# One fused attention and two-MoE kernel: a batch's attention cut in two token halves, weight preparation and two small routing pieces put at other places of the order

## The chip, the cores and the metric

The kernel runs on one core of a Trainium2 chip. The metric is the device time of one execution, in microseconds (us). The same launch holds all three parts of the reference, so there is one time for all of it. PE is the matrix engine (TensorE), DVE the vector engine, ACT the scalar engine, POOL is GpSimd, and SP is the engine whose queue issues most transfers. Every engine works off its instructions in the order in which the program lists them; what comes later on an engine waits behind what comes earlier.

## The reference

Three stages follow each other. Attention reads 4 batches of 8 heads with 512 tokens and 32 state rows of 64 numbers; the tokens read the state and the state reads the tokens:

```
scores  = scale * x @ state^T     a  = softmax(scores)     xread = a  @ state
scores2 = scale * state @ x^T     a2 = softmax(scores2)    sread = a2 @ x
x = concat([xread, sread], tokens)          # 4 * 544 = 2176 rows of 8*64 = 512
```

The first mixture of experts has 8 experts of width 1024. Its weights P come from a gate after 8 rounds of row and column scaling over all 2176 rows, and every expert works on every row:

```
out = sum over e of P[:, e] * (relu(x @ w1[e]) @ w2[e])
```

The second mixture takes that result. Every row goes to the one expert of its largest gate logit, and the result is scaled by that expert's softmax value and by a sigmoid of a second gate. Everything is float32.

## The kernel before

All matrix products that need float32 precision are made of two parts: a number is written as hi + lo (both in a reduced format, fp32r), and a product is three matmuls, hi·hi, hi·lo and lo·hi. The hi part is a copy on ACT, the lo part a subtraction on DVE or POOL.

**The first mixture** takes most of the time: 3 passes over the rows (768, 768 and 640 of them, held transposed in `xst`), each of 32 steps. A step `s` is a quarter of one expert. `mm1(s)` is a product of two 2×2 block matrices in seven block products instead of eight (p1 to p7; L483 to L485 are the three matmuls of each), and needs seven operands of `x` (`XR`, made once for a pass by `xsplit`, L405 to L407, of four sums that `xsums` makes, L390 to L393) and seven of the weights (made for each step by `prep_w1`: f0 are four sums on POOL, L433 to L436, and two copies on ACT, L437 and L438; f1 is a cast on ACT, L441, and the lo parts on POOL, L443 to L448, and then the load of the next step's quarter of W1). `prep_w2` casts the step's quarter of W2 (ACT L458), makes its lo part (POOL L461, in two pieces) and then issues the next quarter's load. The results of `mm1` are summed from PSUM on DVE (L509 to L533), made positive on ACT (L492) and split on DVE (L496). `mm2` multiplies these by W2 (L565 to L567) and adds to `acc` (DVE L583).

**The start-up** comes before step 0. The first pass needs the first 768 columns of the transposed attention result, which is all of batch 0 and the first 256 tokens of batch 1. The start-up computes batches 0 and 1 entirely, in five links for each batch and each half of the heads: c1 transposes x (PE L202, copies ACT L205 and DVE L207), c2 makes scores (PE L213; DVE, ACT), c3 scales (DVE L230 to L233), c4 transposes the result (PE L238, copy ACT L240) and c5 multiplies with the state (PE L250; copies into `xst` at L254 and, for the columns that belong to the second pass, into `xtm` at L256, from where they go to DRAM). Between the links, and between the block products of step 0, PE runs products of ones (`idle_work`, L138), which compute nothing that is used.

**A queue** holds what is left of the attention (batches 2 and 3, the reads of the states, the gate L310 of each row tile), and then the row and column scaling (`sinkhorn`). `pump` takes items from it at fixed places of the steps: each place brings as much credit as the PE work there lasts, and an item costs `pace`. So the list's order and `pace` set at which place of which step an item's instructions stand on every engine. ACT, DVE, POOL and SP get them at the same places.

**The second mixture** begins behind the third pass. `sel_a` (L731 to L750) is an item of the queue in the third pass and works out on DVE which rows go to the first two slots. The tail runs slots: `m1`, `hT` (transposes; copies L877 on ACT and the lo part L878 on DVE), `m2s` (L885 to L887; result scaled on DVE L891 and scattered by POOL L892). `split_w` splits the next slot's weights (ACT L810, DVE L811 of 128x2048 each). `Rq[3][2]` and `Rq[4][2]` are the small operations of `fc` (L697 to L708, 11 each), `gmul` makes `osg` of their result on POOL (L1208, two operations), and `gtab` (PE L719, then DVE L1216) multiplies by it; `gt` scales the results of slots from 2 on.

The order within each engine is written by hand: the body stands under `tc.manual_schedule()`, so the order of the calls is the order of the instructions.

Of the kernel before, what the change touches and what calls it, by code (L numbers as in the profile page):

```python
# [21 lines left out]
def tile_state_attention_moe_moe2(  # L22
# [166 lines left out]
    def attention(b, g):  # L189
# [3 lines left out]
        def c1():  # L193
            xb = xbs.pop((b, g))
            if b == 1:
                T["xT"] = acc.rearrange("p a c -> p (a c)")[:, 1024 * g : 1024 * g + 1024].rearrange("p (a s) -> p a s", a=2)
            else:
                T["xT"] = ap2.tile([P, 2, S], F32, tag="xT", name=f"xT{n}")
            for pl in range(2):
                ps = bank(f"psx{n}{pl}")  # L200
                for r in range(R):
                    nc.tensor.transpose(ps[:, r * P : (r + 1) * P],  # L202
                                        xb[:, r, 2 * pl : 2 * pl + 2, :].rearrange("p h d -> p (h d)"), ident)
                if pl == 0:
                    nc.scalar.copy(T["xT"][:, pl, :], ps)  # L205
                else:
                    nc.vector.tensor_copy(T["xT"][:, pl, :], ps)  # L207

        def c2():
            ps = bank(f"pss{n}")  # L210
            for pl in range(2):
                for r in range(R):
                    nc.tensor.matmul(ps[:, r * P + 64 * pl : r * P + 64 * pl + 64],  # L213
                                     T["xT"][:, pl, r * P : (r + 1) * P],
                                     sbds[b][:, g, 64 * pl : 64 * pl + 64], start=True, stop=True)
            m1 = ap2.tile([P, 16], F32, tag="m1", name=f"m1{n}")
            v = ps.rearrange("p (a s) -> p a s", s=NS)
            nc.vector.tensor_reduce(out=m1, in_=v, axis=AX.X, op=ALU.max)
            e1 = ap2.tile([P, S], F32, tag="e1", name=f"e1{n}")
            ev = e1.rearrange("p (a s) -> p a s", s=NS)  # L220
            nc.vector.tensor_tensor(out=ev, in0=v, in1=m1.unsqueeze(2).to_broadcast([P, 16, NS]), op=ALU.subtract)
            nc.scalar.activation(out=e1, in_=e1, func=AF.Exp, scale=SCALE)
            s1 = ap2.tile([P, S], F32, tag="s1", name=f"s1{n}", bufs=4)
            nc.scalar.copy(s1, ps)
            T["s1"], T["e1"] = s1, e1

        def c3():
            d1 = ap2.tile([P, 2, 16], F32, tag="d1", name=f"d1{n}")
            ev = T["e1"].rearrange("p (a s) -> p a s", s=NS)
            nc.vector.tensor_reduce(out=d1[:, 0, :], in_=ev, axis=AX.X, op=ALU.add)  # L230
            nc.vector.tensor_scalar_add(d1[:, 0, :], d1[:, 0, :], EPS)
            nc.vector.reciprocal(d1[:, 1, :], d1[:, 0, :])
            nc.vector.tensor_tensor(out=ev, in0=ev, in1=d1[:, 1, :].unsqueeze(2).to_broadcast([P, 16, NS]), op=ALU.mult)  # L233

        def c4():
            ps = bank(f"psa{n}")
            for r in range(R):
                nc.tensor.transpose(ps[:, r * P : (r + 1) * P], T["e1"][:, r * P : (r + 1) * P], ident)  # L238
            T["aT"] = T["xT"][:, 1, :]
            nc.scalar.copy(T["aT"], ps)  # L240

        def c5():

            c0 = b * S
            n1 = max(0, min(S, 2 * HW - c0))
            if n1 < S:
                xm = xtm[b, g] = ap2.tile([P, 2, S], F32, tag="xtm", name=f"xtm{n}")
            for pl in range(2):
                po = bank(f"pso{n}{pl}")
                nc.tensor.matmul(po, stps[b][64 * pl : 64 * pl + 64, g, :], T["aT"][64 * pl : 64 * pl + 64, :],  # L250
                                 start=True, stop=True)
                kt = 2 * g + pl
                if n1 > 0:
                    nc.scalar.copy(XT1[:, kt, c0 : c0 + n1], po[:, 0:n1])  # L254
                if n1 < S:
                    nc.vector.tensor_copy(xm[:, pl, n1:], po[:, n1:])  # L256
            if n1 < S:
                o = c0 + n1 - 2 * HW
                nc.sync.dma_start(out=xtd[:, 2 * g : 2 * g + 2, o : o + S - n1], in_=xm[:, :, n1:])
# [1023 lines left out]
```

## Time and profile before

| what | value |
|---|---|
| median of 3 runs | 1806.25 us (1804.05 to 1806.64) |
| the profiled execution's own time | 1801.52 us |
| span of its trace | 1799.8 us |
| PE busy | 1770.6 us, 98% |
| DVE, POOL, ACT busy | 67%, 63%, 36% |
| granted PE clock, mean | 0.996 |

The span is the time from the first to the last instruction in the trace; 1.7 us of the execution's own time lie around it. A granted clock of 1.00 is 2.4 GHz and one of 0.50 is 1.2 GHz. In a timeline a row gives start, duration, engine, line, operation, operands and shape; xN says that N of them follow each other, and the bracket says how long the engine was idle ahead of it and what ended that. A matmul's duration includes its passage through the array, so matmuls overlap: the distance of two starts is what one costs.

### The profile page before, as it was taken

The page shows a single profiled execution, that of the slowest core. Times are in us where ns is not written, and L with a number is a line of the kernel's source. Part 1 is how long each engine was busy: PE and PEld are TensorE (multiplying, and loading weights), DVE is VectorE, ACT ScalarE, POOL GpSimd, SP SyncE. Part 2 cuts the span into 40 slices and gives each one's busy share as a digit, 9 for nine tenths or more (in the row PEclk, how much of TensorE's full clock was granted, in tenths as well). Part 3 has the DMA queues.
Part 4 walks back from the last instruction along what each step waited for, and adds up shares of the span by engine and source line. Part 5 has one row for each costly group of instructions (what it writes and reads, how often), then busy time and mean ns, then how long its engine had stood idle before and what let it go on. Part 6 is the DMA issues. An engine that isn't in the chain of part 4 may idle for free.

```text
span 1799.8 us, 25885 instructions
## 1 busy us (share of the span) xinstructions
PE 1770.6 (98%) x9415; PEld 1579.6 (88%) x9415; DVE 1202.5 (67%) x2054; ACT 654.3 (36%) x1114; POOL 1126.4 (63%) x1045
## 2 busy tenths in 40 slices
PE   8999999999999999999999999999999999999998
PEld 6888999999999889999999999889999998778886
DVE  6667589976666786666666666896666666635232
ACT  4433333333333433333333334333333334336333
POOL 2643566876866766666668776787878887311212
PEclk9999999999999999999999999999999999999999
DMA  5342222222222322222232223242222222434122
GB/s 123 89 111 85 79 69 71 71 74 93 68 71 68 122 70 70 70 61 69 71 100 71 71 69 96 71 141 83 82 82 83 82 76 77 138 115 176 43 92 86
DMA packets 126620, 154.67 MB, mean 86 GB/s; under 512 B 41424, under 2 KB 91600, under 8 KB 123920
## 3 DMA queue, kind: packets, MB, share of 16 engines
q1 hardware_dynamic: 122560, 142.55, 25.3%
q0 software_dynamic: 3280, 10.23, 1.8%
q8 instruction: 76, 1.25, 0.3%
q14 instruction: 64, 0.52, 0.1%
q10 hardware_dynamic: 640, 0.13, 0.0%
HBM read 138.99 MB, written 14.42 MB: 85 GB/s over the span
## 4 chain that ended last, share of the span: by engine, by line
PE 77%; issue 10%; DMA 5%; DVE 4%; POOL 2%; ACT 1%; SPq 0%; POOLq 0%; DVEq 0%; ACTq 0%
PE py L565 13%; PE py L566 13%; PE py L567 13%; PE p L483 11%; PE p L485 11%; PE p L484 11%; DMA out_dram<-xst,si 2%; DMA out_dram<-y,si 2%; PE psr L288 1%; PE psg L310 1%; DVE acc L583 1%; POOL wl L461 1%; DMA xb<-in_x_dram 1%; PE pl L612 0%; DVE HB L496 0%
## 5 line engine op out<-in xcount | busy, mean ns | idle before, releaser
L461 POOL TENSOR_TENSOR wl<-rawb,wh 128x512 fp32r<-128x512 f32 x192 | 247.5, 1311 | 395.3 <-ACT wh L458 393.7
L483 PE MATMUL p<-XR 128*128 128x384 f32 (+1 forms) x1344 | 443.7, 330 | 2.6 <-DVE acc L583 2.3
L484 PE MATMUL p<-XR 128*128 128x384 f32 (+1 forms) x1344 | 439.6, 327 | 4.5 <-POOL XR L407 3.9
L485 PE MATMUL p<-XR 128*128 128x384 f32 (+1 forms) x1344 | 439.7, 327 | 0.8 <-POOL XR L448 0.8
L565 PE MATMUL py<-wh,HB 128*128 128x512 f32 x1088 | 428.3, 394 | 1.0 <-DVE u L515 0.8
L567 PE MATMUL py<-wh,HB 128*128 128x512 f32 x1088 | 425.0, 391 | 0.0
L566 PE MATMUL py<-wl,HB 128*128 128x512 f32 x1088 | 424.9, 391 | 0.0
L583 DVE SCALAR_TENSOR_TENSOR acc<-py,PG,acc 128x512 f32<-128x512 f32 x461 | 320.3, 739 | 53.0 <-PE py L567 52.3
L448 POOL TENSOR_TENSOR XR<-sst,XR 128x512 fp32r<-128x512 f32 x192 | 273.6, 1445 | 31.1 <-ACT XR L441 29.8
L484 PEld LDWEIGHTS p<-XR 128*128 128x128 f32 x1344 | 253.2, 188 | 8.8 <-POOL XR L407 4.3
L483 PEld LDWEIGHTS p<-XR 128*128 128x128 f32 x1344 | 253.1, 188 | 7.8 <-DVE acc L583 2.7
L485 PEld LDWEIGHTS p<-XR 128*128 128x128 f32 x1344 | 252.9, 188 | 1.4 <-POOL XR L448 1.4
L565 PEld LDWEIGHTS py<-wh,HB 128*128 128x128 f32 x1088 | 204.4, 188 | 43.2 <-DVE u L515 0.9
L567 PEld LDWEIGHTS py<-wh,HB 128*128 128x128 f32 x1088 | 204.2, 188 | 43.3
L496 DVE SCALAR_TENSOR_TENSOR HB<-u,HB 128x384 fp32r<-128x384 f32 (+1 forms) x192 | 161.8, 845 | 119.1 <-ACT HB L492 118.9
L566 PEld LDWEIGHTS py<-wl,HB 128*128 128x128 f32 x1088 | 204.4, 188 | 38.7
L501 ACT COPY u<-p 128x384 f32<-128x384 f32 (+1 forms) x96 | 44.3, 461 | 462.0 <-PE p L485 461.9
L443 POOL TENSOR_TENSOR XR<-rawb,XR 128x512 fp32r<-128x512 f32 x96 | 140.3, 1461 | 0.4 <-ACT XR L437 0.4
L441 ACT CAST XR<-sst 128x1024 fp32r<-128x1024 f32 x96 | 100.7, 1048 | 101.2 <-POOL sst L436 101.1
L492 ACT ACTIVATE HB<-u 128x384 fp32r<-128x384 f32 (+1 forms) x192 | 96.8, 504 | 77.3 <-DVE u L528 72.1
L509 DVE TENSOR_TENSOR u<-p,u 128x384 f32<-128x384 f32 (+1 forms) x96 | 51.2, 533 | 93.5 <-PE p L485 93.5
L492 ACT ACTIVATE HB<-p 128x384 fp32r<-128x384 f32 (+1 forms) x96 | 45.4, 473 | 164.5 <-PE p L485 164.5
(304 smaller groups left out, 2492.0 us busy)
## 6 DMA issues: line engine op xcount, KB each, us to landing
rawb<-in_moe_w_dram SPq DMA_DIRECT2D x192, 512.0 KB, 3.5
raw<-in_moe_w_dram SPq DMA_DIRECT2D x15, 1024.0 KB, 7.9
xb<-in_x_dram SPq DMA_DIRECT2D x60, 128.0 KB, 3.5
rawb<-in_moe_w_dram SPq DMA_DIRECT2D x5, 1024.0 KB, 5.1
x1d<-acc SPq DMA_DIRECT2D x16, 256.0 KB, 4.3
xtd<-xtm SPq DMA_DIRECT2D x4, 512.0 KB, 2.7
x1p<-acc SPq DMA_DIRECT2D x8, 256.0 KB, 4.3
xst<-xtd SPq DMA_DIRECT2D x1, 1536.0 KB, 9.4
```

Of the source, the lines that this page charges most:

```text
L443: nc.gpsimd.tensor_tensor(out=wop(s, 1, 0, 2).rearrange(r, k=KD), in0=raw[:, :, 0:P], in1=wop(s, 0, 0, 2).rearrange(r, k=KD).bitcast(F32), ...
L448: nc.gpsimd.tensor_tensor(out=wop(s, 1, 3 + i, 2), in0=sst[:, i : i + 2, :].rearrange("p a c -> p (a c)"), in1=wop(s, 0, 3 + i, 2).bitcast ...
L461: nc.gpsimd.tensor_tensor(out=lo[:, c], in0=raw[:, c], in1=hi[:, c].bitcast(F32), op=ALU.subtract)
L483: nc.tensor.matmul(ps, wh, xh, start=start and k == 0, stop=False, skip_group_check=True)
L484: nc.tensor.matmul(ps, wh, xl, start=False, stop=False, skip_group_check=True)
L485: nc.tensor.matmul(ps, wl, xh, start=False, stop=stop and k == 1, skip_group_check=True)
L492: nc.scalar.activation(out=hh[:, f, half * h : (half + 1) * h], in_=c, func=AF.Relu)
L496: nc.vector.scalar_tensor_tensor(out=hl[:, f, q], in0=c, scalar=0.0, in1=hh[:, f, q].bitcast(F32), op0=ALU.max, op1=ALU.subtract)
L565: nc.tensor.matmul(ps, hh[:, j, r], whi[:, j, :], start=(j == 0), stop=False)
L566: nc.tensor.matmul(ps, hh[:, j, r], wlo[:, j, :], start=False, stop=False)
L567: nc.tensor.matmul(ps, hl[:, j, r], whi[:, j, :], start=False, stop=(j == 1))
L583: nc.vector.scalar_tensor_tensor(out=a, in0=ps, scalar=PG[:, t, e : e + 1], in1=a, op0=ALU.mult, op1=ALU.add)
```

## The change

Five edits.

1. `attention` is written as parts over ranges of tokens. Batch 1 is cut in two halves; the start-up computes only the first half of its tokens, and the second half's ten closures stand at the head of the queue, before batch 2. For that x of batch 1 is loaded a second time at the end of the start-up, in place of batch 2, whose load has become part of queue items, as has the state of batch 3. The gates are taken in another order.
2. The start-up and step 0 have another order. Before: `w1b` (the second half of `prep_w1(0)`) behind A1[3]; now between A0[2] and A1[2]. Both halves of `prep_w1(1)` now stand in step 0 or before it, and `prep_w2(0)` at the place 5 of step 0 and not at the place 1. One lo part of `x` (operand 3) moves from POOL to DVE. There are 12 more products of ones in the start-up and 4 fewer in step 0.
3. The pace of the queue is 108 over its 74 items, before 104 over 64.
4. `sel_a` is cut in two items of the queue, `sel_a` and `sel_a2`.
5. In the tail `Rq[3][2]`, `Rq[4][2]` and `gmul` are called behind `hT(1)`; before, they stood inside `m2s(0)`.

```diff
-    def attention(b, g):
+    def attention(b, g, cuts=(0, R)):
...
+        def part(r0, r1):
+            Q = {}
+            nr = r1 - r0
+            w, c = nr * P, slice(r0 * P, r1 * P)
...
+            def c1():
+                xb = xbs.pop((b, g))
+                if b == 1 and r0 == 0:
+                    xt = accf[:, 1024 * g : 1024 * g + 1024]
                 else:
+                    xt = ap2.tile([P, 2 * S], F32, tag="xT", name=f"xT{m}")
...
+        reads = [part(r0, r1) for r0, r1 in zip(cuts, cuts[1:])]
...
-        pool = (3, 1, 6) if p > 0 else (3, 2)
+        pool = (3, 1, 6) if p > 0 else (2,)
...
+        sel.update(o1=o1, tw=tw, es=es)
+
+    def sel_a2():
+        o1, tw = sel["o1"], sel["tw"]
...
-                crit[b, g], lag[b, g] = attention(b, g)
+
+                reads, lag[b, g] = attention(b, g, (0, R) if b != 1 else (0, R // 2, R))
+                crit[b, g] = reads[0]
+                late[b, g] = reads[-1]
...
-        idle_work(6)
+        idle_work(8)
         C0[0]()
+        idle_work(4)
         C1[0]()
         w1a, w1b = prep_w1(0)
         w1a()
         A0[2]()
+        w1b()
         A1[2]()
         C0[1]()
-        idle_work(4)
+        idle_work(10)
         A0[3]()
         idle_work(6)
         A1[3]()
-        w1b()
         C1[1]()
...
-        early = {0: [parts[2], parts[3]], 4: [sums[2]], 1: [parts[4], sums[3]], 2: [parts[5], parts[6]]}
+        ahead_w1 = prep_w1(1)
+        ahead_w1[0]()
+        early = {0: [parts[2]], 4: [parts[3], ahead_w1[1], parts[5]], 1: [sums[2], parts[4], sums[3]], 2: [parts[6]]}
...
-            ahead = s > 0 and s % NU == 0
+            ahead = s % NU == 0
...
-                    idle_work((4, 4, 4, 4, 12, 4, 0)[i])
-                if i == 1 and not ahead:
+                    idle_work((4, 4, 4, 4, 8, 4, 0)[i])
+                if i == (1 if s > 0 else 5) and (s == 0 or not ahead):
                     prep_w2(s)
...
-            load_x(2, g)
+            load_x(1, g)
         load_state(2)
-        load_state(3)
...
-        queue += spread(window(2), [6, 7, 0, 1, 2, 3, 4, 5], 2)
+        h0, h1 = late[1, 0], late[1, 1]
+        queue += spread([h0[0], h1[0], h0[1], seq(lambda: load_x(2, 0), h1[1]), h0[2], seq(lambda: load_x(2, 1), h1[2]),
+                         h0[3], h1[3], h0[4], seq(h1[4], lambda: load_state(3))], [0, 1, 2, 3], 2)
+        queue += spread(window(2), [6, 7, 4, 5], 2)
...
-        pace[0] = 104.0 / len(queue)
+        pace[0] = 108.0 / len(queue)
...
-        m2s(0, (None,) * 6 + (btab, seq(lambda: gather(2), Rq[3][2], Rq[4][2], gmul)))
+        m2s(0, (None,) * 6 + (btab, lambda: gather(2)))
         hT(1)
+        Rq[3][2]()
+        Rq[4][2]()
+        gmul()
         gather(3)
```

Three places show what this does to the order of an engine. The changed file has more lines, so a line of before has another number after: L407 is L424, L433 to L436 are L450 to L453, L443 to L448 are L460 to L465, L458 is L475, L461 is L478, L492 is L509, L501 is L518, L811 is L832, L878 is L899, L891 is L912.

First POOL, from the first sums of W1 (`sst`) on. `wl` is the lo part of W2, `XR` with `sst` or `rawb` beside it the lo parts of W1, `XR` with `acc` or `xst` beside it the lo parts of x. Before:

```order
L433 TENSOR_TENSOR sst<-rawb 128x256
...
L443 TENSOR_TENSOR XR<-rawb,XR 128x512
L445 TENSOR_TENSOR XR<-rawb,XR 128x256
L448 TENSOR_TENSOR XR<-sst,XR 128x512 x2
L407 TENSOR_TENSOR XR<-acc,XR 128x768
L461 TENSOR_TENSOR wl_522<-rawb,wh_521 128x512 x2
L407 TENSOR_TENSOR XR<-xst,XR 128x768
L433 TENSOR_TENSOR sst<-rawb 128x256
```

And after, from the same place on:

```order
L450 TENSOR_TENSOR sst<-rawb 128x256
...
L465 TENSOR_TENSOR XR<-sst,XR 128x512 x2
L450 TENSOR_TENSOR sst<-rawb 128x256
...
L465 TENSOR_TENSOR XR<-sst,XR 128x512 x2
L424 TENSOR_TENSOR XR<-xst,XR 128x768
L478 TENSOR_TENSOR wl_556<-rawb,wh_555 128x512 x2
L478 TENSOR_TENSOR wl_590<-rawb,wh_589 128x512 x2
```

The lo part of `acc` has left POOL, the lo part of `xst` stands ahead of W2's and no longer behind it, and all of step 1's W1 work stands ahead of both.

Then ACT, from the end of step 0 into step 1. `wh` is the cast of a quarter of W2 (the first is step 0's, the second step 1's), `HB` the hi parts of mm1's results, `xT` the transposed x of an attention link. Before:

```order
L492 ACTIVATE HB<-c_106 128x384
L492 ACTIVATE HB<-u_105 128x384
L441 CAST XR<-sst 128x1024
L492 ACTIVATE HB<-u_104 128x384
L501 COPY u_103<-p_1_598 128x384
L458 CAST wh_614<-rawb 128x1024
L437 CAST XR<-rawb 128x512
L438 CAST XR<-rawb 128x256
L205 COPY xT_647<-psx_648 128x512
```

And after:

```order
L509 ACTIVATE HB<-c_106 128x384
L509 ACTIVATE HB<-u_105 128x384
L475 CAST wh_555<-rawb 128x1024
L509 ACTIVATE HB<-u_104 128x384
L518 COPY u_103<-p_1_573 128x384
L475 CAST wh_589<-rawb 128x1024
L215 COPY xT_2_595<-psx_20_596 128x256
L215 COPY xT_2_612<-psx_20_613 128x256
```

Step 0's cast of W2 has come down to the end of step 0, step 1's is behind it by two instructions, and two copies of the new queue items stand right behind that.

Last DVE in the tail. Before (`xst` from `pY` is the result of slot 0, `HB` the lo part of slot 1's `hT`, `setb` the lo part of slot 2's weights):

```order
L705 TENSOR_TENSOR rt_g<-rt_mx,rt_s 128x2
L707 CAST gsplit<-rt_g 128x2
L708 TENSOR_TENSOR gsplit<-rt_g,gsplit 128x2
L891 TENSOR_SCALAR xst<-pY_14162,gt 128x512
L878 TENSOR_TENSOR HB<-pt_0_14242,HB 128x512
L878 TENSOR_TENSOR HB<-pt_1_14249,HB 128x512
...
L811 TENSOR_TENSOR setb_14270<-rawb,HB 128x2048
```

And after:

```order
L912 TENSOR_SCALAR xst<-pY_14227,gt 128x512
L899 TENSOR_TENSOR HB<-pt_0_14282,HB 128x512
L899 TENSOR_TENSOR HB<-pt_1_14289,HB 128x512
L714 TENSOR_REDUCE rt_s<-rt_d 128x3
L715 TENSOR_SCALAR rt_s<-rt_s 128x3
...
L724 CAST gsplit<-rt_g 128x2
L725 TENSOR_TENSOR gsplit<-rt_g,gsplit 128x2
L832 TENSOR_TENSOR setb_14335<-rawb,HB 128x2048
L714 TENSOR_REDUCE rt_s<-rt_d 128x3
L715 TENSOR_SCALAR rt_s<-rt_s 128x3
...
L724 CAST gsplit<-rt_g 128x2
L725 TENSOR_TENSOR gsplit<-rt_g,gsplit 128x2
L832 TENSOR_TENSOR setb_14335<-rawb,HB 128x2048
L714 TENSOR_REDUCE rt_s<-rt_d 128x3
L715 TENSOR_SCALAR rt_s<-rt_s 128x3
...
L724 CAST gsplit<-rt_g 128x2
L725 TENSOR_TENSOR gsplit<-rt_g,gsplit 128x2
L832 TENSOR_TENSOR setb_14335<-rawb,HB 128x2048
```

The 22 operations of the two `fc` stood ahead of these rows and now stand behind them, ahead of the first L832 of slot 2's weights.

## Rows read from the trace of the kernel before

**Rows 1.** The page, busy time of the engines (share of the span, instructions).

```profile
PE 1770.6 (98%) x9415; PEld 1579.6 (88%) x9415; DVE 1202.5 (67%) x2054; ACT 654.3 (36%) x1114; POOL 1126.4 (63%) x1045
```

**Rows 2.** Waits of PE by tile, line and releaser; total us, times, longest.

```profile
PE p L484 <- POOL XR L407: 3.9, 1, 3.9
PE pY L887 <- DVE HB L878: 3.7, 2, 3.4
PE p L483 <- DVE acc L583: 2.3, 2, 1.9
```

**Rows 3.** Timeline of PE, 0 to 50 us.

```profile
32.34 1.99 PE L250 MATMUL pso<-acc,stp 64*128 64x512 f32 x8
34.26 0.44 PE L483 MATMUL p<-XR 128*128 128x384 f32 x1
```

**Rows 4.** Timeline of PE, 50 to 80 us.

```profile
53.71 0.52 PE L483 MATMUL p<-XR 128*128 128x384 f32 x1
...
57.62 0.33 PE L483 MATMUL p<-XR 128*128 128x384 f32 x1
...
58.66 1.03 PE L202 MATMUL psx<-ident,xb 128*128 128x128 f32 x8
...
73.20 1.90 PE L213 MATMUL pss<-sbd,xT 128*128 128x64 f32 x16
```

**Rows 5.** Timeline of POOL, 14 to 75 us.

```profile
27.64 2.95 POOL L448 TENSOR_TENSOR XR<-sst,XR 128x512 fp32r<-128x512 f32 x2 [6.96 <-ACT XR L441]
38.78 1.87 POOL L407 TENSOR_TENSOR XR<-acc,XR 128x768 fp32r<-128x768 f32 x1 [8.20 <-ACT XR L405]
43.41 3.92 POOL L461 TENSOR_TENSOR wl<-rawb,wh 128x512 fp32r<-128x512 f32 x2 [2.75 <-ACT wh L458]
47.29 1.80 POOL L407 TENSOR_TENSOR XR<-xst,XR 128x768 fp32r<-128x768 f32 x1
```

**Rows 6.** Timeline of DVE, 26 to 66 us.

```profile
34.58 0.95 DVE L390 TENSOR_TENSOR acc<-xst 128x768 f32<-128x768 f32 x1
...
38.88 2.59 DVE L392 TENSOR_TENSOR acc<-xst 128x768 f32<-128x768 f32 x1
```

**Rows 7.** Timeline of ACT, 34 to 66 us.

```profile
42.29 1.04 ACT L458 CAST wh<-rawb 128x1024 fp32r<-128x1024 f32 x1
...
51.74 0.52 ACT L492 ACTIVATE HB<-u 128x384 fp32r<-128x384 f32 x1 [3.93 <-DVE u L528]
...
59.30 0.59 ACT L205 COPY xT<-psx 128x512 f32<-128x512 f32 x1 [0.71 <-PE psx L202]
```

**Rows 8.** The page, weight quarter loads: queue, count, size, us to landing.

```profile
rawb<-in_moe_w_dram SPq DMA_DIRECT2D x192, 512.0 KB, 3.5
```

**Rows 9.** Timeline of DVE, 1146 to 1158 us.

```profile
1153.55 2.05 DVE L583 SCALAR_TENSOR_TENSOR acc<-py,PG,acc 128x512 f32<-128x512 f32 x3
```

**Rows 10.** Timeline of DVE, 1562 to 1584 us.

```profile
1563.49 0.17 DVE L697 TENSOR_REDUCE rt_s<-rt_d 128x3 f32<-128x24 f32 x1
...
1568.16 1.28 DVE L878 TENSOR_TENSOR HB<-pt,HB 128x512 fp32r<-128x512 f32 x2
1569.66 2.29 DVE L811 TENSOR_TENSOR setb<-rawb,HB 128x2048 fp32r<-128x2048 f32 x1 [0.23 <-issue]
```

**Rows 11.** Timeline of POOL, 1562 to 1584 us.

```profile
1567.47 1.71 POOL L1208 TENSOR_TENSOR osg<-sm,gsplit 128x408 fp32r<-128x408 bf16 x2 [3.14 <-DVE gsplit L707]
```

**Rows 12.** Timeline of PE, 1563 to 1584 us.

```profile
1575.63 1.97 PE L719 MATMUL pgat<-osg,ohj 128*128 128x48 f32 x17
...
1579.59 0.58 PE L862 MATMUL pm<-HB,XR 128*128 128x512 f32 x1
```

**Rows 13.** Three stretches: length, busy time (instructions) by engine, clock, DMA, GB/s.

```profile
47.20:54.00 6.80, 4.86 (x16) 4.37 (x17) 1.33 (x4) 1.98 (x3) 6.72 (x8) 0.51 0.23 77
1154.40:1157.00 2.60, 2.60 (x14) 2.30 (x15) 2.50 (x6) 0.00 (x0) 2.52 (x3) 1.00 0.28 106
1579.00:1583.00 4.00, 4.00 (x11) 2.84 (x12) 2.34 (x2) 2.23 (x2) 1.74 (x2) 0.61 0.81 306
```

More of the change, by code (lines that the diff above doesn't have):

```diff
@@ L187, in tile_state_attention_moe_moe2 @@
     xtm = {}
-    def attention(b, g):
+    accf = acc.rearrange("p a c -> p (a c)")
+    def attention(b, g, cuts=(0, R)):
         n = f"{b}{g}"
         T = {}
[L193 to L205, printed above, removed]
-                else:
[L207 to L259, printed above, removed]
@@ L295, in n3 @@
                 nc.scalar.copy(xs[q, 2 * g : 2 * g + 2, NS * b : NS * b + NS], pv[q, :, NS * par : NS * par + NS])
-        return [c1, c2, c3, c4, c5], [n1_, n2, n3]
+        return reads, [n1_, n2, n3]
     def gate(ts):
@@ L751, in sel_a @@
                                     in1=ids[:, 0:NP].unsqueeze(2).to_broadcast([P, NP, 2]), op=ALU.mult)
-        sel.update(o1=o1, tw=tw, es=es, os0=os0, osr=osr, osg=osg)
+        sel.update(os0=os0, osr=osr, osg=osg)
     R2 = [rawb.rearrange("p a c -> p (a c)"), None, None, None]
@@ L912, in tile_state_attention_moe_moe2 @@
     with tc.manual_schedule():
-        accf = acc.rearrange("p a c -> p (a c)")
-        crit, lag = {}, {}
+        crit, lag, late = {}, {}, {}
         for b in range(B):
             for g in range(G):
-                crit[b, g], lag[b, g] = attention(b, g)
+                reads, lag[b, g] = attention(b, g, (0, R) if b != 1 else (0, R // 2, R))
+                crit[b, g] = reads[0]
+                late[b, g] = reads[-1]
         constants()
@@ L1110, in tile_state_attention_moe_moe2 @@
             if s == 2 * NU + 1:
-                queue += [Rq[1][0]] + rest_(2) + [Rq[1][1]] + rest_(1) + [seq(Rq[1][3], sel_a)] + rest_(1) + [Rq[1][2], Rq[2][0]] + rest_(1) + [
+                queue += [Rq[1][0]] + rest_(2) + [Rq[1][1]] + rest_(1) + [seq(Rq[1][3], sel_a), sel_a2] + rest_(1) + [Rq[1][2], Rq[2][0]] + rest_(1) + [
                     sel_b] + rest_(2) + [sel_c, load_first, Rq[2][1], first_rows, Rq[2][2]]
```

62 lines of the change are left out of this document (added).

## The prediction, made before the changed kernel ran

> **What bounds the kernel now.** I read the page's busy times first: PE works for 1770.6 us of the 1799.8 us span [rows 1], every other engine far less, so the end moves only if PE gets less to do, waits less, or runs less at the lower clock. The change takes no product of the reference away, so I went next to the list of PE's waits. Three of them are of single places that the diff touches: 3.9 us for a lo part of x on POOL, 3.4 us for a lo part of slot 1 on DVE, and 1.9 us (the longest of two) for a DVE addition in the third pass [rows 2]. Then the timeline of PE from 0 to 80 us: the first block product stands at 34.26 [rows 3], the first of step 1 at 53.71 [rows 4]. In steps 1 and 2, to which work moves, PE's rows follow each other without a wait: there is nothing to remove there, only something to add.
>
> **The 3.9 us wait.** POOL works on in order: lo part of `acc` at 38.78, two pieces of W2's lo part from 43.41 for 3.92, and only then the lo part of `xst`, 47.29 to 49.09, for which PE waits [rows 5]. In the new order that lo part stands ahead of W2, and the one at 38.78 is gone to DVE. What replaces it is another chain. W1's second lo parts (two of them 2.95 when nothing disturbs them) now run from about 18.3, beside the scaling of batch 0; step 1's W1 work stands ahead of the lo part of `xst` too.
>
> How the engines disturb each other: DVE's difference L390 takes 0.95 us, the like operation L392 takes 2.59, when it starts 0.1 us after a POOL operation of 1.87 [rows 5, 6]; its end lies 0.82 behind POOL's end, so it did its work after POOL. And the two POOL pieces take 3.92 in place of 2.95 beside DVE operations with two inputs in SBUF. So I let such pairs follow each other. Beside that: "SBUF — State Buffer" of the Trainium skill, section "SBUF: two separate sides", calls the port pair of the two engines an exclusive lock; by it what POOL now does ahead of step 0's end keeps the DVE sums waiting in full, and without it my replay has step 1 start 2 us earlier than I write below; L392 agrees with it.
>
> I replayed the new orders with the durations of the rows. The start-up has half of batch 1 less: last copy into `xst` 3.1 us earlier, at 31.9; first product at 31.4 instead of 34.26, −2.9. Then p2, p6 and p5 gain 2.9 to 3.6 each. The sums of x wait for POOL's step 1 work (until 39.0), the fifth operand's lo part is there at 41.0, the third's (POOL) at 42.65 instead of 49.09, and the last (DVE) at 45.4. p4 is last and ends at 46.3; that is where step 1 begins, before at 53.71: **−7.4**. Before, about 0.5 us more was lost to slow products behind 53.71 (0.52 each there, 0.33 at 57.62 [rows 4]), which I add: **−0.5**. Bounds: the wait and the clock gone and nothing in their place, −9.4; DVE and POOL alternating for 3 us more, −4.4. The products of ones (12 more, 4 fewer, about 0.1 us each) stand in gaps in which PE waits for DVE or DMA; where they don't, they cost 0.9, which is inside this range.
>
> **What comes back: moved work.** The second half of batch 1 now runs inside steps 1 and 2, where PE has no gaps: eight transpositions (1.03), sixteen score products (1.90), four transpositions (half of 1.03) and four products with the state of half the width of those that took 1.99 [rows 3, 4]. With the passage that each duration holds taken off, **+3.9** (between 3.4 and 4.5). Its x is loaded twice; that is 1 MB on a queue with room.
>
> **What comes back: new waits.** ACT is in order. At the end of step 0 it makes the result of p3 positive (0.52), then casts W2(0) (1.04), later W2(1), and right behind that copies the transposed x of the late half (half of 0.59, as the shape is half) [rows 7]. W2(1) can land only after W2(0)'s lo part on POOL has read its buffer. Chain: u4 at 46.85, positive at 47.4, cast to 48.4, POOL's two pieces (2.95) to 51.35, load 3.5 [rows 8] to 54.8, cast W2(1) to 55.85, copy to 56.15. PE comes to the scores of that half after 36 matmuls of step 1 (six in 1.04 us [rows 4], so 6.3), eight transpositions and a gate, at about 54.35: it waits **+1.85**. At the low end PE comes there 1.85 later, held up by a disturbed step 0, and the wait is 0; at the high end POOL's pieces take the disturbed 3.92 [rows 5] and the load 1 us more, and it is 4. Queued behind that cast stand the next quarter's W1 casts and the exponentials; their delay lets the two later transpositions of the links wait 0.95 and 0.6 in my replay: **+1.55** (0 to 3).
>
> Sum of the start: −7.4 − 0.5 + 3.9 + 1.85 + 1.55 = **−0.6**; most of the removed wait is paid back. From step 3 on the queue is only denser (1.46 us of PE work an item, before 1.63), and no wait was near: 0 (up to +1). The scaling's last item slides one step, to directly ahead of the first product whose addition needs it; PSUM has banks enough to hide about 1 us of DVE there: 0.
>
> **The 1.9 us wait.** It ends when three additions, which start only at 1153.55, behind the operations of `sel_a` [rows 9], free a bank. Cut in two with an addition between, DVE frees it in time: **−1.5** (−1.9 to 0).
>
> **The tail.** `fc` twice ran on DVE from 1563.49 to 1567.5, ahead of `hT(1)`'s lo part, which PE waited for [rows 2, 10]. It goes behind: PE resumes at 1565.5, −3.4, and slot 1 is done by 1570.5. What is late next: `fc` ends at 1570.0, POOL's first `osg` piece (0.85, half of 1.71 [rows 11]) at 1570.7, DVE's L811 (2.29 [rows 10]) holds the second until 1573.0, `osg` is there at 1573.85. The table's product starts there, before at 1575.63 [rows 12]. The weights of slot 2 go on as fast as their loads, then slot 1's result, then the copy of x: the first products of slot 2 come to 1577.7 where they were at 1579.59 [rows 12]: **−1.9** (−0.4 to −3.5).
>
> Here the clock matters. In 47.2 to 54.0 the granted clock is 0.51, behind PE's wait of 3.9 us, and in 1579 to 1583 it is 0.61, behind waits ahead of slot 2; in 1154.4 to 1157, behind the wait of 1.9 us in the third pass, it is full [rows 2, 13]. A stretch of 6.8 us at 0.51 loses 3.3 us, 4 us at 0.61 lose 1.6. I leave the second loss in the tail as it is, since PE now waits 3.3 us (1570.5 to 1573.85) ahead of the table. The Trainium skill's "TensorE: Matmul & The Clock Gate", section "HAM oscillation — how this bites in real kernels", shows a matmul kernel that falls to the lower clock at each of its waits for DMA; if the new wait of 1.85 us did that, the start would lose 1.6 us more. The row at 1154.4 speaks against it for a wait of this size, the row at 47.2 for it from 3.9 us on.
>
> **Sum:** −0.6 − 1.5 − 1.9 = **−4.0 us** against the profiled 1801.52, so 1797.5; that execution lies 4.7 below the median, so against the median 1806.25 − 4.0 = **1802.3**. A measurement of this kernel can tell about 0.2%, 3.6 us, from no change; my forecast lies at that bound.
>
> **Rivals.** (a) *No change, about −1 us (1805).* The start gains nothing net, the wait for `osg` takes the tail's gain (−0.4), and the third pass keeps half of its wait: +0.5 − 0.4 − 1.0. For it: POOL at the start gets more to do early, and each chain of replacements above is longer than the wait it removes. Against: the three waits are single and named. Chance 0.30. (b) *Slower, about +3 (1809).* One mechanism: the W2(1) load. If it lands after 58 (POOL's W2(0) piece pushed behind DVE and a transfer slowed by the x loads), ACT's queue holds the late half's copies, then `HB` of step 1, then mm2(1); PE waits 5.55 us in step 1 instead of 1.85, and falls to the lower clock as at 47.2: −0.6 + 3.7 for the wait + 3.3 for the clock − 3.4 for the two other places. It decides at a wait of over 4.5 us there. For it: the wait of 3.9 us took the clock down. Against: 192 such loads land after 3.5 us [rows 8]. Chance 0.13. (c) *More, about −9 (1797).* No waits in steps 1 and 2 (−3.4) and full clock in slot 2 (−1.6). For it: the end bounds above. Chance 0.13. My forecast, −2 to −6.5, has 0.44.
>
> Faster by over 0.2%: (c), and about seven tenths of the forecast's part, 0.44; within: 0.40; slower: 0.16, with what else a denser queue may do. The range reaches from (c) to (b): 1796.5 to 1808.5; the forecast's own is 1800 to 1804.5.
>
> **What would show it.** Right: the 3.9 us wait is gone, step 1's first product is near 46, scores of the late half wait 1 to 3 us for ACT, the additions of the third pass start before 1151 in that place, slot 1 has no wait for DVE, and `osg` releases the table's product. Wrong: step 1 begins after 48.5 (alternation dearer), steps 1 and 2 hold over 5 us of waits, a lower clock in them, or `osg` as late as before.

## The result, and the profile after

The change made the kernel slower. In 8 runs each the median went from 1803.60 to 1812.21 us, a ratio of 1.0051 with a 95% interval of 1.0037 to 1.0066: 9.2 us (6.7 to 11.9), where 4.0 us less was forecast. The profiled executions have spans of 1799.8 and 1810.4, so the 10.6 us between them can be read from the traces.

First a ledger. ACT's copy `u<-p` (L501, after L518) stands once in each step of the first mixture. The table gives how much later (us) it starts in a kernel than in the kernel before, for some steps, and for the span's end; the kernels below `after` are the experiments. Each row is one profiled execution, which can lie off its kernel's median: e7's was the fastest of 12 (1799.06 us, median 1801.64), e2's and e5's were 3.5 and 3.7 us above theirs.

| kernel | step 0 | 1 | 16 | 71 | 72 | 95 | end |
|---|---|---|---|---|---|---|---|
| before, start (us) | 35.61 | 55.16 | 345.60 | 1204.78 | 1218.81 | 1517.35 | 1799.8 |
| after | +0.1 | −3.6 | +5.3 | +6.0 | **+12.6** | +12.6 | +10.6 |
| e1, sel_a joined | +0.1 | −3.6 | +4.5 | +4.5 | +4.4 | +4.4 | +3.8 |
| e2, old places | +4.6 | +1.0 | +9.1 | +8.4 | +8.3 | +8.3 | +7.6 |
| e3, start alone | −1.7 | −5.3 | +3.7 | +4.6 | +3.9 | +3.9 | +3.8 |
| e4, tail alone | +0.4 | −0.1 | +0.7 | +1.7 | +1.0 | +1.0 | −0.8 |
| e5, w1b late | +2.9 | −0.8 | +8.2 | +8.2 | +8.1 | +8.1 | +5.9 |
| e6, more ones | −2.7 | −6.4 | +2.6 | +3.5 | +2.8 | +2.8 | +1.1 |
| e7, W2(0) early | −2.4 | −6.1 | −0.7 | +0.2 | −0.5 | −0.5 | −2.4 |
| e8, uncut | +0.5 | −2.3 | −1.2 | −0.2 | −0.9 | −0.9 | −2.1 |
| e9, split alone | +0.1 | −0.5 | +0.4 | +1.0 | **+6.1** | +6.1 | +6.0 |
| e10, empty item | 0.0 | 0.0 | −0.1 | +2.4 | **+7.4** | +7.4 | +7.3 |
| e11, e2 and e7 | −0.8 | −4.5 | +1.0 | +0.4 | +0.4 | +0.4 | −1.0 |
| e12, combined | +0.6 | −2.3 | −3.4 | −3.9 | −3.9 | −3.9 | −5.1 |

Three stretches tell the result. The start gains 3.6 us up to step 1 and loses 8.9 by step 16; 6.6 us are lost in one step of the third pass, between steps 71 and 72, of which the prediction has nothing; and from step 95 to the end 2.0 us are won, as forecast.

The waits of PE in the kernel after (total, times, longest, us), which answer to [rows 2]:

```profile
PE p L500 <- DVE acc L600: 4.1, 3, 2.0
PE p L500 <- ACT u L518: 3.0, 2, 2.8
PE psx L212 <- DMA xb<-in_x_dram: 2.5, 4, 0.7
PE psa L251 <- DVE e L246: 2.5, 2, 1.5
PE pss L223 <- ACT xT L215: 1.7, 1, 1.7
...
PE p L500 <- ACT XR L422: 1.4, 1, 1.4
```

The 3.9 us wait for POOL and the 3.4 us wait for DVE are gone, and so is the one of 1.9 us at its place. In their place stand waits for the additions L600, for ACT's copy of `u`, and of the late half's scores for ACT's `xT`.

**The start.** PE's timeline after:

```profile
24.05 1.12 PE L251 MATMUL psa<-ident,e 128*128 128x128 f32 x4 [1.53 <-DVE e L246]
...
26.69 3.74 PE L263 MATMUL pso<-xT,stp 64*128 64x512 f32 x8
...
34.24 0.44 PE L500 MATMUL p<-XR 128*128 128x384 f32 x1
...
42.85 0.44 PE L500 MATMUL p<-XR 128*128 128x384 f32 x1 [1.40 <-ACT XR L422]
43.93 0.69 PE L501 MATMUL p<-XR 128*128 128x384 f32 x1 [0.64 <-DVE XR L424]
...
49.47 0.33 PE L500 MATMUL p<-XR 128*128 128x384 f32 x1
...
59.36 1.10 PE L223 MATMUL pss<-sbd,xT 128*128 128x64 f32 x8 [1.70 <-ACT xT L215]
```

Eight products with the state take 3.74 us where eight such products took 1.99 [rows 3]: the granted clock is 0.52 there (first row below). The first block product stands at 34.24, no earlier than before; step 1's stands at 49.47 (before 53.71 [rows 4]). The granted clock (the column after POOL's busy time) in the stretches concerned:

```profile
24.00:30.50 6.50, 6.45 (x22) 3.84 (x23) 3.85 (x12) 3.43 (x9) 2.83 (x4) 0.52 0.71 140
...
44.00:47.50 3.50, 3.50 (x13) 3.00 (x14) 3.07 (x3) 0.83 (x1) 1.55 (x1) 0.52 0.00 0
...
60.90:65.30 4.40, 4.40 (x19) 3.82 (x19) 3.52 (x7) 1.06 (x3) 4.32 (x6) 0.61 0.43 119
...
1212.00:1216.00 4.00, 1.99 (x10) 1.73 (x9) 3.93 (x7) 1.06 (x3) 3.92 (x5) 0.84 0.17 59
1216.00:1220.00 4.00, 3.17 (x15) 2.91 (x14) 3.82 (x8) 0.44 (x1) 3.96 (x5) 0.74 0.35 131
1220.00:1226.00 6.00, 5.10 (x18) 4.33 (x19) 5.84 (x13) 1.50 (x3) 0.00 (x0) 0.72 0.27 90
```

**The third pass.** The 1.9 us wait has gone from its place, but another stands 13 us behind it. ACT waits for DVE's routing operations, and its copy of `u`, for which PE waits, stands behind that:

```profile
1171.03 0.23 ACT L667 ACTIVATE rt_d<-rt_d 128x32 f32<-128x32 f32 x1 [7.39 <-DVE rt_d L666]
1171.75 0.41 PE L500 MATMUL p<-XR 128*128 128x320 f32 x1 [2.77 <-ACT u L518]
```

The larger loss follows. POOL and DVE after, between steps 71 and 72. L859 is a gather of rows for the second mixture, L460 to L465 are W1's lo parts, L513 splits mm1's results, L600 adds mm2's.

```profile
1204.95 1.17 POOL L859 DMA_INDIRECT xst<-x1p,gi  x1 [0.18 <-DVE rt_rb L703]
1206.42 0.99 POOL L859 DMA_INDIRECT xst<-x1p,gi  x1 [0.31 <-issue]
1207.44 1.30 POOL L460 TENSOR_TENSOR XR<-rawb,XR 128x512 fp32r<-128x512 f32 x1
1208.70 1.01 POOL L462 TENSOR_TENSOR XR<-rawb,XR 128x256 fp32r<-128x256 f32 x1
1209.68 2.54 POOL L465 TENSOR_TENSOR XR<-sst,XR 128x512 fp32r<-128x512 f32 x2
```

```profile
1209.44 4.61 DVE L513 SCALAR_TENSOR_TENSOR HB<-u,HB 128x320 fp32r<-128x320 f32 x2
1213.97 1.40 DVE L600 SCALAR_TENSOR_TENSOR acc<-py,PG,acc 128x512 f32<-128x512 f32 x2
1215.29 0.17 DVE L714 TENSOR_REDUCE rt_s<-rt_d 128x4 f32<-128x32 f32 x1
...
1220.02 0.17 DVE L725 TENSOR_TENSOR gsplit<-rt_g,gsplit 128x4 fp32r<-128x4 f32 x1
1220.10 2.06 DVE L600 SCALAR_TENSOR_TENSOR acc<-py,PG,acc 128x512 f32<-128x512 f32 x3
```

```profile
1214.77 0.64 PE L500 MATMUL p<-XR 128*128 128x320 f32 x1 [2.01 <-DVE acc L600]
1220.90 0.42 PE L500 MATMUL p<-XR 128*128 128x320 f32 x1 [1.73 <-DVE acc L600]
```

The two gathers hold POOL from 1204.95 to 1207.44 between W1's sums and its lo parts. The lo parts then run beside DVE's last splits of the step, and two splits take 4.61 us; before, the two took 0.48 and 1.30:

```profile
1203.61 0.48 DVE L496 SCALAR_TENSOR_TENSOR HB<-u,HB 128x320 fp32r<-128x320 f32 x1
1204.81 1.30 DVE L496 SCALAR_TENSOR_TENSOR HB<-u,HB 128x320 fp32r<-128x320 f32 x1 [0.71 <-ACT HB L492]
```

The additions behind them are late, and between them stand the 11 operations of an `fc` for 4.9 us. PE pays 2.01 and 1.73 for it. The 14 us from 1212 on have a clock of 0.72 to 0.84, which is about 3.4 us lost to a full clock by the last three rows of the clock table above (an estimate). By the ledger the whole is 6.6: the two waits make 3.7 of it, the clock most of the rest. Before, the gathers stood at another place of POOL's order:

```profile
1188.32 2.78 POOL L448 TENSOR_TENSOR XR<-sst,XR 128x512 fp32r<-128x512 f32 x2 [1.73 <-ACT XR L441]
1191.28 1.17 POOL L838 DMA_INDIRECT xst<-x1p,gi  x1 [0.18 <-DVE acc L583]
1192.76 1.47 POOL L838 DMA_INDIRECT xst<-x1p,gi  x1 [0.31 <-issue]
1194.25 2.58 POOL L461 TENSOR_TENSOR wl<-rawb,wh 128x512 fp32r<-128x512 f32 x2
```

There they stand behind the lo parts of W1, ahead of W2's, and no wait of PE follows before 1205.

**The tail.** PE, DVE and POOL after, which answer to [rows 10 to 12]; all that stands ahead of the gain is 12.6 us later than before:

```profile
1584.07 2.08 PE L736 MATMUL pgat<-osg,ohj 128*128 128x48 f32 x17 [0.76 <-POOL osg L1236]
1587.41 0.79 PE L881 MATMUL pm<-HB,XR 128*128 128x512 f32 x1 [0.68 <-ACT XR L870]
1590.15 0.79 PE L883 MATMUL pm<-HB,XR 128*128 128x512 f32 x1 [1.52 <-DVE XR L871]
```

```profile
1577.28 1.29 DVE L899 TENSOR_TENSOR HB<-pt,HB 128x512 fp32r<-128x512 f32 x2 [0.30 <-ACT HB L898]
1578.48 0.17 DVE L714 TENSOR_REDUCE rt_s<-rt_d 128x3 f32<-128x24 f32 x1
```

```profile
1582.31 1.71 POOL L1236 TENSOR_TENSOR osg<-sm,gsplit 128x408 fp32r<-128x408 bf16 x2 [4.03 <-DVE gsplit L724]
```

PE's wait of 3.4 us for the lo part of slot 1 is gone: DVE makes that part at 1577.28, as soon as ACT's hi part is there, and `fc` follows. `osg` is what PE waits for next, 0.76 us to 1584.07: 4.1 us less than 12.6 + 1575.63 [rows 12]. It then waits for the copy of x (0.68) and its lo part (1.52). L883 stands at 1590.15, 2.0 us less than 12.6 + 1579.59.

### The profile page after: what moved, and what is told of

Read it like the earlier page. It is cut to its first block, busy times and chain, and to the rows that moved or that the text cites. A ratio compares the mean times of both kernels' runs of the same rounds, so it can differ in the third digit from the quotient of the medians.

```text
span 1810.4 us, 25948 instructions
## 1 busy us (share of the span) xinstructions
PE 1778.9 (98%) x9431; PEld 1584.2 (88%) x9431; DVE 1206.2 (67%) x2069; ACT 655.5 (36%) x1122; POOL 1126.6 (62%) x1044
## 4 chain that ended last, share of the span: by engine, by line
PE 75%; issue 10%; DVE 6%; DMA 5%; POOL 3%; ACT 1%; SPq 1%; POOLq 0%; DVEq 0%; ACTq 0%
PE py L582 12%; PE py L583 12%; PE py L584 12%; PE p L500 11%; PE p L502 11%; PE p L501 11%; DMA out_dram<-xst,si 2%; DMA out_dram<-y,si 2%; DVE HB L513 1%; PE psr L305 1%; POOL wl L478 1%; DVE acc L600 1%; PE psg L327 1%; PE pss L223 1%; POOL XR L424 1%
## 5 line engine op out<-in xcount | busy, mean ns | idle before, releaser
L478 POOL TENSOR_TENSOR wl<-rawb,wh 128x512 fp32r<-128x512 f32 x192 | 246.0, 1303 | 408.7 <-ACT wh L475 408.7
L501 PE MATMUL p<-XR 128*128 128x384 f32 (+1 forms) x1344 | 440.0, 327 | 0.6 <-DVE XR L424 0.6
L600 DVE SCALAR_TENSOR_TENSOR acc<-py,PG,acc 128x512 f32<-128x512 f32 x461 | 320.4, 740 | 53.2 <-PE py L584 52.5
L465 POOL TENSOR_TENSOR XR<-sst,XR 128x512 fp32r<-128x512 f32 x192 | 273.0, 1441 | 34.0 <-ACT XR L458 34.0
L501 PEld LDWEIGHTS p<-XR 128*128 128x128 f32 x1344 | 253.6, 189 | 4.1 <-DVE XR L424 0.9
L513 DVE SCALAR_TENSOR_TENSOR HB<-u,HB 128x384 fp32r<-128x384 f32 (+1 forms) x192 | 163.0, 850 | 119.3 <-ACT HB L509 118.9
L518 ACT COPY u<-p 128x384 f32<-128x384 f32 (+1 forms) x96 | 44.3, 461 | 451.7 <-PE p L502 451.7
L460 POOL TENSOR_TENSOR XR<-rawb,XR 128x512 fp32r<-128x512 f32 x96 | 139.2, 1450 | 8.4 <-ACT XR L454 8.4
L458 ACT CAST XR<-sst 128x1024 fp32r<-128x1024 f32 x96 | 100.7, 1049 | 106.1 <-POOL sst L453 106.0
L509 ACT ACTIVATE HB<-u 128x384 fp32r<-128x384 f32 (+1 forms) x192 | 96.8, 504 | 81.6 <-DVE u L545 69.3
L509 ACT ACTIVATE HB<-p 128x384 fp32r<-128x384 f32 (+1 forms) x96 | 45.5, 474 | 171.6 <-PE p L502 171.6
```

What stands on the lines that cost most here:

```text
L460: nc.gpsimd.tensor_tensor(out=wop(s, 1, 0, 2).rearrange(r, k=KD), in0=raw[:, :, 0:P], in1=wop(s, 0, 0, 2).rearrange(r, k=KD).bitcast(F32), ...
L465: nc.gpsimd.tensor_tensor(out=wop(s, 1, 3 + i, 2), in0=sst[:, i : i + 2, :].rearrange("p a c -> p (a c)"), in1=wop(s, 0, 3 + i, 2).bitcast ...
L478: nc.gpsimd.tensor_tensor(out=lo[:, c], in0=raw[:, c], in1=hi[:, c].bitcast(F32), op=ALU.subtract)
L501: nc.tensor.matmul(ps, wh, xl, start=False, stop=False, skip_group_check=True)
L509: nc.scalar.activation(out=hh[:, f, half * h : (half + 1) * h], in_=c, func=AF.Relu)
L513: nc.vector.scalar_tensor_tensor(out=hl[:, f, q], in0=c, scalar=0.0, in1=hh[:, f, q].bitcast(F32), op0=ALU.max, op1=ALU.subtract)
```

## Experiments

The theory after the trace: the extra queue item, by its place, costs 6.6 us; the start loses by the moved half and by ACT's wait in it; the tail is right. The rivals: that the clock in the start-up is the start's loss, that the two pieces of `sel_a` cost by themselves, or that all hangs on the phase of a changed start. All comparisons are with the kernel before on the same chip; e1 to e4, e5 to e8 and e9 to e12 ran on three chips, so a comparison across these groups is one of ratios.

**e1: sel_a in one item again.** In the changed kernel:

```diff
-... + [seq(Rq[1][3], sel_a), sel_a2] + rest_(1) + ...
+... + [seq(Rq[1][3], sel_a, sel_a2)] + rest_(1) + ...
```

> The changed kernel with sel_a and sel_a2 joined again in one queue item; all else as changed. Theory: the extra item moved the gathers and the last fc of the third pass one place later, and 6.6 us of the loss (between steps 71 and 72) come from that, so it runs about 6.6 us under the changed kernel, some 2 us over the kernel before, the 1.9 us wait at the second addition is back, and no wait of 2.0 and 1.7 us stands between steps 71 and 72. Rival: the loss there comes from the shifted phase of the start and tail, then it stays within 2 us of the changed kernel.

Measured: median 1804.51 against 1802.14, ratio 1.0014 (1.0004 to 1.0024), +2.5 us where the changed kernel has +9.2: 6.7 less. Between steps 71 and 72 nothing is lost any more (ledger), and the 1.90 us wait is back, from 1156.9 on.

**e2: two items, later items at their old places.**

```diff
-... + [seq(Rq[1][3], sel_a), sel_a2] + rest_(1) + [Rq[1][2], ...
+... + [seq(Rq[1][3], sel_a), sel_a2] + [Rq[1][2], ...
```

> The changed kernel with sel_a still in two items, but one empty item behind them taken out, so that all later items of that queue keep their old places. Theory (the shift is dear, the split itself is free): like the joined version, 6 to 7 us under the changed kernel, and perhaps 0 to 2 us better still, since the wait of 1.9 us is gone. Rival (two pieces beside POOL's work are dear): it stays at the changed kernel's time.

Measured: 1805.64 against 1802.14, 1.0015 (1.0003 to 1.0026), +2.7 us, like e1. So it is the place of the later items; the split itself costs nothing that can be told. Its profiled execution had a low clock early (0.61 from 14 to 24 us), so its row of the ledger tells only differences between steps. In its trace the gathers stand behind W1's lo parts again:

```profile
1196.71 2.79 POOL L465 TENSOR_TENSOR XR<-sst,XR 128x512 fp32r<-128x512 f32 x2 [1.73 <-ACT XR L458]
1199.68 1.16 POOL L859 DMA_INDIRECT xst<-x1p,gi  x1 [0.17 <-DVE acc L600]
1201.15 1.46 POOL L859 DMA_INDIRECT xst<-x1p,gi  x1 [0.31 <-issue]
1202.64 2.55 POOL L478 TENSOR_TENSOR wl<-rawb,wh 128x512 fp32r<-128x512 f32 x2
```

The gain of the split is small: between steps 67 and 71 this profile wins 0.6 us on the kernel before, since the wait of 1.9 us is gone and one of 0.8 has come.

**e9: the split alone, in the kernel before; e10: no split, but one empty item more.**

```diff
-... + [seq(Rq[1][3], sel_a)] + rest_(1) + [Rq[1][2], ...
+... + [seq(Rq[1][3], sel_a), sel_a2] + rest_(1) + [Rq[1][2], ...     (e9)
+... + [seq(Rq[1][3], sel_a)] + rest_(2) + [Rq[1][2], ...             (e10)
```

> The kernel before with sel_a in two items of the queue alone. Theory (the extra item moves the two gathers and the last fc of that queue one place later): 6 to 7 us over the kernel before, with PE waits near 2 us between steps 71 and 72. Rival (that loss needs the changed start): within 2 us of the kernel before.

> The kernel before with sel_a in one item and one empty item more behind it, so that the later items stand where the split puts them. Theory (the places alone cost, not the split): 6 to 7 us over the kernel before, like the split alone. Rival (two pieces of sel_a are what costs): the kernel before's time.

Measured: e9 1807.69 against 1802.23, 1.0036 (1.0023 to 1.0049), +6.5 us; e10 1809.41, 1.0045 (1.0032 to 1.0058), +8.1. An item that does nothing costs as much: the place alone does it, without the changed start. The median granted clock of their executions is 0.994 and 0.995, that of the kernel before 0.995, so little of this goes with the clock. By the ledger e10 loses 5.0 us between steps 71 and 72 and 2.4 ahead of them, where the wait for `u` has come while the 1.9 us wait has stayed; e1 and e2 have no such wait for `u`. So the added item costs at both places, and in the changed kernel the first eats what the split of `sel_a` wins. Which of the shifted items (the routing, the gathers, `fc`) costs how much was not run apart. The two waits of PE in e10 that have grown, as in the changed kernel (the additions, before 2.3 [rows 2], and the copy of `u`):

```profile
PE p L483 <- DVE acc L583: 5.6, 3, 2.0
...
PE p L483 <- ACT u L501: 2.5, 1, 2.5
```

**e4: the tail's edit alone, in the kernel before.**

```diff
-        m2s(0, (None,) * 6 + (btab, seq(lambda: gather(2), Rq[3][2], Rq[4][2], gmul)))
+        m2s(0, (None,) * 6 + (btab, lambda: gather(2)))
         hT(1)
+        Rq[3][2]()
+        Rq[4][2]()
+        gmul()
```

> The kernel before with the tail's edit alone (the two fc and gmul behind hT(1)). Theory: 2.0 us faster than the kernel before, as from step 95 to the end in the changed kernel. Rival (the gain there came from a later phase of the loads): 0.

Measured: 1800.68 against 1802.14, 0.9992 (0.9981 to 1.0003), −1.4 us; the interval touches zero, but the trace has the same 1.8 us between step 95 and the end as the changed kernel (2.0), and the eight other experiments with this tail win 0.7 to 2.2 there; e3, e9 and e10, with the tail of before, 0.1.

**e3: the start, the queue and the pace alone** (the changed kernel with e1's line and the tail of before).

> The kernel before with the start-up, the queue and its pace of the changed kernel alone (sel_a in one item, tail as before). Theory: the start-up gives back 3.6 us up to step 1 and loses 8.9 us by step 16 (moved work 3.9, a wait of 1.7, two stretches at half clock), so about 5 us slower than the kernel before. Rival (queue density alone, no clock): 0 to 2 us slower.

Measured: 1806.03 against 1802.14, 1.0020 (1.0009 to 1.0030), +3.6 us. With e9's +6.5 and e4's −1.4 this makes +8.7 of the +9.2: the parts add up, as far as intervals of some 2 us to either side can tell.

**e8: batch 1 uncut.** In e1, with the reordered start-up and the tail; the loads at the end of the start-up and the pace are those of before too:

```diff
-... = attention(b, g, (0, R) if b != 1 else (0, R // 2, R))
+... = attention(b, g, (0, R))
...
-        queue += spread([h0[0], h1[0], h0[1], ...
-        queue += spread(window(2), [6, 7, 4, 5], 2)
+        queue += spread(window(2), [6, 7, 0, 1, 2, 3, 4, 5], 2)
```

> The joined version with batch 1 not cut: all of its attention in the start-up and the queue and pace of the kernel before; the reordered start-up, step 0 and the tail stay. Theory (the moved half costs 4.1 us in steps 1 and 2 and its wait 1.45, while its removal from the start-up saves 2.9 us at most and risks the clock): step 1 is reached 2 to 3 us under the kernel before, nothing is lost after it, and with the tail it is 3 to 4 us under the kernel before. Rival (the reordering itself loses): not under the kernel before.

Measured: 1800.88 against 1801.91, 0.9992 (0.9983 to 1.0001), −1.4 us; 4.0 less than e1. Against the kernel before, 3 to 4 less was expected, and the interval touches zero; against e1 the moved half, with its loads and its waits, shows: in the ledger e1 loses 8.1 us between steps 1 and 16, e8 1.1, with a new wait of 1.3 for a copy on DVE in it.

What the moved half costs can be counted in the traces. PE's time from the start of one instruction to the next, summed by tile between the copies of steps 1 and 16, before and in e1: scores 6.81 and 8.54, products with the state 4.24 and 5.50, transpositions of x 3.16 and 3.87, of the scaled scores 1.42 and 1.78: 4.1 us together. The block products and those of `mm2` take 4.3 us more. The waits of 1.45, 0.65, 0.44 and 0.37 are in that, and 1.3 us are left without them, which the counted 4.1 don't hold (0.8 in e7).

**e7: W2(0) at place 1 of step 0 again** (in e1).

```diff
-if i == (1 if s > 0 else 5) and (s == 0 or not ahead):
+if i == 1 and (s == 0 or not ahead):
```

> The joined version with step 0's W2 work back at place 1 of step 0. Theory (ACT's in-order cast of W2(1) makes the late half's scores wait 1.45 us): that wait is gone, and POOL's two pieces run before the lo part of operand 5's successor, which costs up to 1 us in step 0; time 0.5 to 1.5 us under the joined version. Rival (POOL's two pieces again stand ahead of a lo part of x): a wait of 2 to 4 us in step 0 and 1 to 3 us over the joined version.

Measured: 1801.64 against 1801.91, 1.0003 (0.9993 to 1.0013); 0.0011 or 2.0 us less than e1, but the two intervals overlap. The traces show the mechanism: the cast stands at 40.27, the next quarter's at 50.77 and not at 57.99 as in the changed kernel, PE has no wait for the late half's scores, and between steps 1 and 16 e7 loses 5.4 us where e1 loses 8.1.

**e6: more products of ones; e5: w1b at its old place** (both in e1).

```diff
-        idle_work(10)
+        idle_work(20)          (e6)
         A0[3]()
-        idle_work(6)
+        idle_work(20)          (e6)
         A1[3]()
+        w1b()                  (e5; taken out ahead of A1[2])
```

> The joined version with 20 products of ones in place of 10 and 20 in place of 6 ahead of the two transpositions of batch 0's scaled scores, where PE waited 1.0 and 1.5 us. Theory (the clock falls because PE has gaps there): PE's clock is full from 24 to 30.5 us in each profile, step 0's copy is reached at about 33.9 and not at 35.7; time 1 to 1.5 us under the joined version. Rival (the clock there does not hang on those gaps, or the ones delay the chain): same time or up to 1 us more.

> The joined version with the second half of step 0's W1 work (w1b) back behind A1[3] in the start-up. Theory (POOL's early lo parts hold up DVE's scaling of batch 0, PE then waits 1.5 us and its clock falls from 24 to 30 us): the wait of 1.5 us at the transposition falls to 0.5, the clock stays full, step 0 is reached 1 to 2 us earlier; time 1 to 2 us under the joined version. Rival (the late lo parts are needed by the first products): the same time or 1 us more.

Measured: e6 1804.23 against 1801.91, 1.0016 (1.0008 to 1.0025), the same as e1; e5 1803.66, 1.0007 (0.9997 to 1.0018), no difference from e1 that can be told. In e5's profile the wait at the transposition is still 1.4 us and the clock is 0.61 from 14 to 24 us, so it does not bear out its theory. e6's profile does what the theory wanted, the clock is full and step 0 is reached 2.8 us earlier than in e1's:

```profile
14.00:24.00 10.00, 9.17 (x82) 7.96 (x81) 8.06 (x15) 4.15 (x9) 8.03 (x9) 1.00 0.80 178
24.00:30.50 6.50, 5.21 (x35) 3.10 (x33) 4.51 (x13) 6.10 (x14) 2.48 (x4) 1.00 0.58 121
```

But e3, whose start-up has the instructions of e1's, had the full clock there too, without more ones, and its step 0 at 33.95 (e1: 0.52 and 35.66):

```profile
24.00:30.50 6.50, 5.12 (x34) 3.38 (x34) 4.56 (x13) 5.04 (x12) 2.82 (x4) 1.00 0.77 157
```

So the fall at 24 us is not a property of the order alone: it differs between executions of the same instructions. Filling PE's gaps with ones did not move the median. e6's profile was its third fastest of 12 (1802.63 us).

The mean granted clock of every timed execution is on record, and the time follows it: of 35 runs of the kernel before, those at 0.992 took 1805.7 to 1806.1 us and those at 0.996 1799.9 to 1802.4, about 1.2 us for each 0.001. The median is 0.994 in e1 and 0.995 in e6, so the more ones do go with a fuller clock, but what that gives is not in e6's time. It is 0.9925 in the changed kernel and 0.995 in the kernel before beside the experiments. By that rate up to 3 of the 9.2 us go with the clock (an estimate: not all the runs of before beside the changed kernel's have a clock on record). How much of that lies in the start-up and how much behind the waits of the third pass, the means don't tell.

**e11 and e12: what the parts make together.** e11 is the changed kernel with e2's and e7's lines; e12 has e8's too.

> The changed kernel with step 0's W2 work back at place 1 and one empty item behind sel_a2 taken out. Theory (the two causes add): about 2 us under the version with the item taken out alone, that is from equal to the kernel before to 1 us under it. Rival (the W2 place matters only with sel_a whole): like the version with the item taken out, 2 to 3 us over the kernel before.

> As the last, and with batch 1 uncut and the queue and pace of before: the reordered start without the moved half, sel_a split without the shift, and the tail. Theory (each part's measured effect adds): 2 to 4 us under the kernel before. Rival (the parts share one gain, as the start-up waits for its data anyway): 1 us under it, like the uncut version.

Measured: e11 1801.29 against 1802.23, 0.9996 (0.9988 to 1.0005), −0.7 us; e12 1796.38, **0.9971** (0.9960 to 0.9983), −5.2 us (−7.2 to −3.1). It beats both kernels; its median clock is 0.997, so by the rate above about half of the gain goes with the clock. In its trace none of the three waits of [rows 2] is left, and no new one over 0.8 us stands in the third pass.

## Why the prediction was wrong, point by point

- **"The 1.9 us wait", −1.5: the step that failed.** "Cut in two with an addition between, DVE frees it in time" came true (0.6 us net, by e2's profile), but an added item also moves all that stands behind it in the queue by one place, and no term and no rival priced that. Measured: +6.5 (e9), and +8.1 for an empty item (e10). The loss does not lie at the 1.9 us wait: it lies with a copy of `u` 13 us later and with gathers and an `fc` 50 us later.
- **The start, −0.6: sign wrong.** Measured: +3.6 (e3, 1.6 to 5.4), of which the moved half with its waits is 4.0 (e8). The moved work (+3.9) was right: 4.1 counted, but the products around it took 0.8 to 1.3 us more too (e7, e1), which was in no term. The late half's wait (+1.85) was right in cause, ACT's in-order cast of W2(1), and in size (1.70; 1.45 in e1). The two later waits of the links (+1.55) hardly came: none over 0.2 in the changed kernel, 0.44 in e1. The replay of the start-up holds where the clock is full from 24 to 30.5 us: first product forecast 31.4, in e6, e7 and e3 31.42, 31.80 and 32.49; step 1 forecast 46.3, there 46.67, 46.95 and 47.76. In the changed kernel's own profile, with 0.52 there, they stand at 34.24 and 49.47, about 3 us later than forecast. What was not in the sum is the low clock behind the late half's wait: 60.9 to 65.3 at 0.61, 1.7 us, in e3 and e6 too but not in e1. And behind step 3, "0 (up to +1)" was 1.0: waits of 0.65 and 0.38. One reading was off without harm: two pieces of POOL take 2.54 to 2.58 undisturbed (rows above), not 2.95.
- **The tail, −1.9: right**, 2.0 in the trace and −1.4 alone (e4), with `osg` next in line as said. But `osg` came about 2.4 us earlier than the replay had it, and PE waited 0.76 us for it and not 3.3; what sets the first products of slot 2 is the copy of x and its lo part, named last in the prediction.
- **The rivals.** Slower by the W2(1) load with the clock behind it (0.13) names a chain that is there, but at 1.7 us of wait and 1.7 of clock, not 5.55 and 3.3; the time came out beyond its 1809, and mostly for another reason. "Wrong if step 1 begins after 48.5" came true (49.47), by the clock of the start-up and not by the alternation that it was to be a sign of.
- **The range** ended at 1808.5, with the kernel before at a median of 1806.25; eight runs put that at 1803.6, so the base of the sum was 2.6 us high; the step of +9.2 would have left the range from either base.

What stays open: what decides the clock in the first 30 us, why e6's median does not gain what its profile gains at the start, and how the cost of the added item divides among the items that it shifts.

## What to carry to other kernels

In an order that a queue deals out by credit, an item's price is where it puts all that comes behind it: compare the order of every engine from there to the queue's end, before pricing the item itself, and give its place back (here one empty item less) when something is cut in two. Work moved out of a start-up that has gaps into steps that have none is paid in full, 4.1 us here, however well the start-up then looks. Where an engine is in order, put a copy for which PE waits ahead of a cast that hangs on a load.
